# One load moves ahead of three others in the load queue: linear attention and two gated layers on one core

## The chip, the cores and the metric

The kernel runs on 1 core of a Trainium2 chip. The metric is the time of one execution on the device in microseconds (us), lower is better. The kernel before took 664.3 us (median of 3 runs, 663.88 to 666.28).

## The reference

Three stages follow each other: linear attention with decays over 4 batches of 8 heads and 768 positions, then two gated feed-forward layers over the 3072 resulting rows of 256.

```python
cum = np.cumsum(la, axis=-1)                      # la = log of the decays a of one chunk
L = np.exp(cum[..., :, None] - cum[..., None, :]) * causal
y = einsum(einsum(C, B) * L, x) + einsum(C, state) * exp(cum)
state = exp(sum(la)) * state + sum_j(B_j x_j * exp(cum[-1] - cum_j))
...
h = sigmoid(y @ w_gate) * (y @ w_val)
z = h @ w_out
...
g = z @ w2_in
out = (g * sigmoid(g)) @ w2_out
```

The reference works in chunks of 32 positions. The kernel takes chunks of 128, which gives the same sums.

## The kernel before

**Attention.** The 4 batches have 6 chunks of 128 positions each, so there are 24 chunks, numbered 0 to 23. For a chunk q the SP queue loads `bc` (B and C), `x` and `L`, the decays of all 8 heads broadcast over 128 partitions (`at_loadL`, L252, 512 KB into an `L` tile of 4 buffers). VectorE (DVE) turns the decays into the matrix L by one scan (`at_L`, L338), and GpSimd (POOL) makes `bw` from its last column (`at_bw`, L346). From chunk 4 on B and C are split in three bf16 parts by POOL (L298, L306), copied into the staging tiles `st` by ScalarE (ACT, L325) and DVE (L323), and transposed by two DMAs of the SP queue (`tr`, L327). TensorE (PE) multiplies the parts to `cb` in two halves (L381), DVE multiplies each half into L (L383), and PE makes `y` (L392 the part from the state, L398 the part within the chunk). ACT and DVE split y into `xT` (L450, L451), the input of the first gated layer.

**First gated layer.** Its 12 weight blocks f (gate, val and out) are loaded raw by three DMAs each (`w1_load`, L198 and L202, into a `raw` tile of 4 buffers), converted (`conv`: ACT L175 and L176, DVE L177 and L178, POOL L183 and L185, ACT L187, DVE L188; for the out part of the first seven blocks also `w1_split`, L221 and L222) and then used by PE (`g`, `v`: L509; `acc`: L558). The rows are taken in 7 row blocks of 2, 2, 4, 4, 4, 4, 4 chunks (`BLOCKS`). Row blocks 0 and 1 run together while the weights arrive; row block 2 (chunks 4 to 7) and later ones have all weights. DVE multiplies gate and value (`sg`, L530).

**Order of the work.** The program is written out by Python lists and then ordered by a scheduler, engine by engine. The SP queue keeps the order in which the loads are written. Two tables set that order: `WPOS` says before which attention step (an index into `ast`) each of the 31 steps of loading, converting and marking weight blocks (`wst`) is put, `RUNS` says how many steps are taken between the matmul groups. A tile's load waits until the last reader of the tile that had its buffer is done.

The lines that the text speaks of: a step with the position 31 is put ahead of attention step 31, one with 32 ahead of step 32.

```python
for i, g in enumerate(ast):
    steps += [w for w, p in zip(wst, WPOS) if p == i] + [g]
```

Of the kernel before, what the change touches and what calls it, by code (L numbers as in the profile page):

```python
# [30 lines left out]


WPOS = [
    0, 0, 0, 22, 25, 31, 31, 31, 31, 31, 31, 31, 32, 32, 32, 32, 32, 32, 32, 32, 32, 34, 34, 34, 34, 34, 35,
    35, 35, 35, 35,
]

# [865 lines left out]
```

## Time and profile before

| what | value |
|---|---|
| median of 3 runs | 664.3 us (663.88 to 666.28) |
| the profiled execution, its own time | 663.99 us |
| its span, first to last instruction | 662.2 us |
| PE busy | 635.5 us (96%) |
| DVE busy | 432.8 us (65%) |
| ACT busy | 329.0 us (50%) |
| POOL busy | 108.7 us (16%) |
| mean granted clock of PE | 0.992 of full speed |

Times in the profile are us from the start of the span. The execution's own time is 1.8 us above the span. Busy time is the sum of an engine's instructions. In the timelines a row is an instruction, or several alike in a row, with its start, how long it lasted, and in brackets how long the engine had stood idle before it and what ended that.

### The profile page before, as it was taken

What the parts mean: (1) busy time and instruction counts of PE and PEld (TensorE: products, weight loads), DVE (VectorE), ACT (ScalarE), POOL (GpSimd) and SP (SyncE); (2) the same over time, 40 slices, a digit from 0 to 9 for tenths busy, and PEclk for the clock granted to TensorE, in tenths of its full rate; (3) what the DMA queues carried; (4) which work ended last, traced back from release to release, by engine and by line L of the source; (5) the groups of instructions that cost most, each with busy time, mean ns of one, the idle gap of its engine ahead of it and who ended that gap; (6) DMA issues with size and microseconds to landing.
All of it is one profiled execution on the core that took longest, in us unless ns stands there. A gap on an engine that the chain in (4) does not pass through costs nothing.

```text
span 662.2 us, 9861 instructions
## 1 busy us (share of the span) xinstructions
PE 635.5 (96%) x3680; PEld 522.0 (79%) x3682; DVE 432.8 (65%) x660; ACT 329.0 (50%) x649; POOL 108.7 (16%) x129
## 2 busy tenths in 40 slices
PE   5788898999999999999999999999999999999998
PEld 2477796777778787787888878888888888888886
DVE  8988987676768578656348885564564655544644
ACT  5675554544544554434336664544554544444543
POOL 4555432211221222311002410000000000000000
PEclk9998999999999999999999999999999999999999
DMA  8958577774656365342002410000000000000000
GB/s 207 267 146 212 89 158 154 153 128 109 120 121 145 77 145 119 81 125 75 0 1 66 157 33 1 1 32 1 1 32 1 1 32 1 33 0 1 33 0 33
DMA packets 140145, 51.18 MB, mean 77 GB/s; under 512 B 119009, under 2 KB 133537, under 8 KB 140097
## 3 DMA queue, kind: packets, MB, share of 16 engines
q1 hardware_dynamic: 139952, 50.41, 32.1%
q8 instruction: 29, 0.48, 0.3%
q14 instruction: 20, 0.16, 0.1%
q10 hardware_dynamic: 144, 0.13, 0.1%
HBM read 36.80 MB, written 3.24 MB: 60 GB/s over the span
## 4 chain that ended last, share of the span: by engine, by line
PE 79%; DVE 4%; DMA 4%; issue 3%; POOL 2%; ACT 1%; SPq 0%; DVEq 0%; POOLq 0%; ACTq 0%
PE h L509 20%; PE o L807 13%; PE v L509 11%; PE acc L558 11%; PE g L509 11%; PE o L828 7%; DMA raw<-in_moe_w_out_dram 3%; PE y L398 2%; DMA L<-ac_d 1%; POOL cvt L185 1%; PE cb L381 1%; PE y L392 1%; DVE sg L530 1%; DVE cvt L178 1%; DVE L L338 1%
## 5 line engine op out<-in xcount | busy, mean ns | idle before, releaser
L509 PE MATMUL v<-xT,w 128*128 128x512 f32 (+1 forms) x504 | 119.4, 369 | 3.9 <-ACT sg L522 2.4
L509 PE MATMUL g<-xT,w 128*128 128x512 f32 (+1 forms) x504 | 120.8, 370 | 0.0
L782 DVE TENSOR_TENSOR sh<-h,sh 128x512 f32<-128x512 f32 x96 | 66.2, 691 | 63.2 <-ACT sh L781 61.7
L509 PE MATMUL h<-x2T,w2b 128*128 128x512 f32 x432 | 107.0, 389 | 0.0
L791 DVE TENSOR_TENSOR gl<-sh,gh 128x512 fp32r<-128x512 f32 x96 | 65.8, 690 | 58.4 <-ACT gh L786 56.9
L509 PEld LDWEIGHTS v<-xT,w 128*128 128x128 f32 x504 | 87.4, 192 | 19.3 <-ACT sg L522 3.0
L509 PEld LDWEIGHTS g<-xT,w 128*128 128x128 f32 x504 | 87.7, 191 | 16.3 <-issue 1.5
L558 PE MATMUL acc<-gh,w 128*128 128x512 f32 (+1 forms) x280 | 94.5, 380 | 0.2 <-ACT x1T L569 0.2
L781 ACT ACTIVATE sh<-h 128x512 f32<-128x512 f32 x96 | 57.5, 599 | 73.3 <-PE h L509 70.2
L509 PEld LDWEIGHTS h<-x2T,w2b 128*128 128x128 f32 x432 | 80.7, 188 | 16.5
L786 ACT CAST gh<-sh 128x512 fp32r<-128x512 f32 x96 | 59.0, 620 | 62.2 <-PE o L807 31.0
L503 ACT CAST gh<-sg 128x512 fp32r<-128x512 f32 (+1 forms) x70 | 41.2, 588 | 93.6 <-DVE sg L530 93.6
L807 PE MATMUL o<-w2b,gh 128*128 128x512 f32 x280 | 74.2, 390 | 0.0
L530 DVE TENSOR_TENSOR sg<-v,sg 128x512 f32<-128x512 f32 (+1 forms) x84 | 50.8, 607 | 30.4 <-PE v L509 29.5
L539 DVE TENSOR_TENSOR gl<-sg,gh 128x512 fp32r<-128x512 f32 (+1 forms) x70 | 50.6, 723 | 23.3 <-ACT gh L503 23.0
L338 DVE TENSOR_TENSOR_SCAN L<-L,eye 128x1024 f32<-128x1024 f32 x24 | 55.2, 2302 | 16.0 <-DMA L<-ac_d 15.9
L185 POOL TENSOR_TENSOR cvt<-cvt,raw 128x512 int32<-128x512 int32 (+1 forms) x28 | 46.5, 1664 | 98.7 <-DVE cvt L178 81.5
L522 ACT ACTIVATE sg<-g 128x512 f32<-128x512 f32 (+1 forms) x84 | 44.8, 534 | 31.5 <-PE g L509 28.6
L558 PEld LDWEIGHTS acc<-gh,w 128*128 128x128 f32 x280 | 52.3, 190 | 9.9 <-ACT x1T L569 0.3
L807 PEld LDWEIGHTS o<-w2b,gh 128*128 128x128 f32 x280 | 51.8, 188 | 10.3
L558 PE MATMUL acc<-gl,w 128*128 128x512 f32 (+1 forms) x140 | 53.3, 380 | 1.0 <-DVE gl L539 1.0
L828 PEld LDWEIGHTS o<-w2b,gl 128*128 128x128 f32 x288 | 36.9, 191 | 1.3
(95 smaller groups left out, 724.9 us busy)
## 6 DMA issues: line engine op xcount, KB each, us to landing
L<-ac_d SPq DMA_DIRECT2D x23, 512.0 KB, 4.7
raw<-in_moe_w_out_dram SPq DMA_DIRECT2D x28, 256.0 KB, 3.9
raw<-in_moe_w_in_dram SPq DMA_DIRECT2D x16, 256.0 KB, 2.8
x<-in_x_dram SPq DMA_DIRECT2D x24, 128.0 KB, 3.1
raw<-in_moe_w_gate_dram SPq DMA_DIRECT2D x12, 256.0 KB, 4.4
raw<-in_moe_w_val_dram SPq DMA_DIRECT2D x12, 256.0 KB, 4.7
out_dram<-o2t SPq DMA_DIRECT2D x20, 128.0 KB, 1.7
bc<-in_B_dram SPq DMA_DIRECT2D x24, 64.0 KB, 2.7
```

What stands on the lines that cost most here:

```text
L185: nc.gpsimd.tensor_tensor(ti, ti, r, ALU.add)
L338: nc.vector.tensor_tensor_scan(t["Lf"], t["Lf"], eye, 0.0, op0=ALU.mult, op1=ALU.add)
L509: nc.tensor.matmul(psum[:, :n], w[:, i, o + k * P : o + (k + 1) * P], xt[j][:, k, :n], start=(z == 0), stop=(z == len(k_terms) - 1),)
L530: nc.vector.tensor_mul(sg[:, :n], ps[:, :n], sg[:, :n])
L539: nc.vector.tensor_sub(lo[:, :n], sg[:, :n], hi[:, :n].bitcast(F32))
L558: mm = nc.tensor.matmul(o, v[:, ms], g[:, :n], start=(f == 0 and z == 0 and not (small and m)), stop=(f == NF1 - 1 and z == len(terms) - 1 ...
L781: nc.scalar.activation(sg, ps, AF.Sigmoid)
L782: nc.vector.tensor_mul(sg, ps, sg)
L786: nc.scalar.copy(hi, sg)
L791: nc.vector.tensor_sub(lo, sg, hi.bitcast(F32))
L807: nc.tensor.matmul(ps, hi[:, s], w2(f)[:, :, DM:], start=(f == 0), stop=False, skip_group_check=True,)
L828: nc.tensor.matmul(ps[:, :DM], g2[b, f][2][:, s], w2(f)[:, 0, DM:], start=False, stop=(f == NF2 - 1), skip_group_check=True,)
```

## The change

Nine numbers of `WPOS` go from 32 to 33.

```diff
 WPOS = [
-    0, 0, 0, 22, 25, 31, 31, 31, 31, 31, 31, 31, 32, 32, 32, 32, 32, 32, 32, 32, 32, 34, 34, 34, 34, 34, 35,
+    0, 0, 0, 22, 25, 31, 31, 31, 31, 31, 31, 31, 33, 33, 33, 33, 33, 33, 33, 33, 33, 34, 34, 34, 34, 34, 35,
     35, 35, 35, 35,
 ]
```

The nine steps are three conversions, three loads and three marks. Attention step 32 is the load of the decays of chunk 4, so that load is now written ahead of them.

The SP queue, from the load of x of chunk 4 on. `x_494` is that x; `L_551` before and `L_505` now is the tile of the decays of chunk 4; `raw_514`, `raw_535`, `raw_547` (now `raw_516`, `raw_537`, `raw_549`) are the weight blocks 7, 8 and 9. Before:

```order
 L273 DMA x_494<-in_x_dram 128x8x32
-L198 DMA raw_514<-in_moe_w_gate_dram 128x2x256
-L198 DMA raw_514<-in_moe_w_val_dram 128x2x256
-L202 DMA raw_514<-in_moe_w_out_dram 128x512
-L198 DMA raw_535<-in_moe_w_gate_dram 128x2x256
-L198 DMA raw_535<-in_moe_w_val_dram 128x2x256
-L202 DMA raw_535<-in_moe_w_out_dram 128x512
-L198 DMA raw_547<-in_moe_w_gate_dram 128x2x256
-L198 DMA raw_547<-in_moe_w_val_dram 128x2x256
-L202 DMA raw_547<-in_moe_w_out_dram 128x512
-L252 DMA L_551<-ac_d 128x1024
+L252 DMA L_505<-ac_d 128x1024
```

The load of the decays stood behind nine load instructions of three weight blocks, and now stands right behind the load of x; the nine follow it in their old order.

The scheduler moves work on the other engines too. DVE, where the scan of chunk 4 stands now (`w_105` are the converted weights, `st` the staging of chunk 4, `cvt_478` the conversion of block 4):

```order
 L178 SCALAR_TENSOR_TENSOR cvt_478<-raw_420,cvt_478 128x768
 L451 TENSOR_TENSOR xT_1_413<-y_432,xT_1_412 128x2x128
+L338 SCALAR_TENSOR_TENSOR L_505<-L_505,eye 128x1024
 L222 TENSOR_TENSOR w_105<-x1T,w_105 128x256
 L188 TENSOR_TENSOR w_105<-cvt_445,w_105 128x512
 L323 COPY st_617<-bc_615 128x8x32
 L323 COPY st_623<-bc_615 128x8x2x16
```

The scan stood 21 instructions further on, behind the conversion of block 7 (`cvt_539`), and now comes ahead of the weight splits and the staging copies of chunk 4. In the same way the scan of chunk 5 (`L_640`) now comes behind the staging copies of that chunk's B and C (`st_668`, `st_674`) instead of ahead of them.

DVE, some 50 instructions later, at the staging copies of chunk 6 (`st_760`, `st_766`) and the scan of chunk 6 (`L_707`):

```order
+L383 TENSOR_TENSOR L_640<-cb_1_722,L_640 128x512
+L338 SCALAR_TENSOR_TENSOR L_707<-L_707,eye 128x1024
+L188 TENSOR_TENSOR w_105<-cvt_598,w_105 128x768
 L530 TENSOR_TENSOR sg_7_1172<-v_7_1174,sg_7_1172 128x256
-L383 TENSOR_TENSOR L_640<-cb_0_709,L_640 128x512
-L188 TENSOR_TENSOR w_105<-cvt_598,w_105 128x768
 L323 COPY st_760<-bc_737 128x8x32
 L323 COPY st_766<-bc_737 128x8x2x16
```

Here the scan went the other way: it stood behind the staging copies of chunk 6, and now stands ahead of them, with the last weight conversion and a gate product between.

On PE the matmuls of the state of chunk 4 (L414) move up, behind the products of row block 1 with weight block 1, and those of `cb` of chunk 5 move up ahead of the gate matmuls of row block 1 with weight block 7. On POOL `bw` of chunk 4 moves up ahead of the conversion of weight block 5. On DVE the second multiply of `cb` into L of chunk 7 (L383) now stands ahead of the low part of `xT` of chunk 6 (L451); both stand behind the scan of chunk 8, and `y` of chunk 7 (L392) waits for that part. After row block 2 the orders are as they were, but for a few rows.

## Rows read from the trace of the kernel before

**Rows 1.** The page, part 1: busy us (share of the span) and instructions.

```profile
PE 635.5 (96%) x3680; PEld 522.0 (79%) x3682; DVE 432.8 (65%) x660; ACT 329.0 (50%) x649; POOL 108.7 (16%) x129
```

**Rows 2.** Busy time by stretch: PE, PEld, DVE, ACT, POOL, then clock, DMA share, GB/s.

```profile
40.00:62.00 22.00, 17.58 (x116) 15.62 (x115) 18.06 (x25) 15.54 (x30) 13.65 (x12) 0.99 0.60 174
62.00:112.00 50.00, 44.40 (x391) 39.89 (x391) 45.07 (x71) 25.07 (x59) 17.21 (x19) 0.94 0.70 136
112.00:350.00 238.00, 238.00 (x1447) 188.86 (x1447) 152.33 (x236) 107.50 (x219) 45.67 (x61) 1.00 0.46 101
```

**Rows 3.** Timeline of PE, two places at which it waited.

```profile
61.04 1.33 PE L509 MATMUL v<-xT,w 128*128 128x256 f32 x6 [2.36 <-ACT sg L522]
...
109.81 0.71 PE L392 MATMUL y<-cwT,S 128*128 128x128 f32 x4 [1.61 <-DVE xT L451]
```

**Rows 4.** Timeline of the SP queue: start, duration of the issue.

```profile
37.13 2.12 SPq L273 DMA_DIRECT2D x<-in_x_dram  x1
43.99 0.37 SPq L198 DMA_DIRECT2D raw<-in_moe_w_gate_dram  x1
...
52.72 0.37 SPq L198 DMA_DIRECT2D raw<-in_moe_w_gate_dram  x1
...
54.15 0.43 SPq L252 DMA_DIRECT2D L<-ac_d  x1
```

**Rows 5.** Tile L, 10 to 125 us: load to landing, min, median, max.

```profile
DMA to landing us min/median/max: 4.2/4.8/6.5
```

**Rows 6.** Timeline of DVE around the old and the new place of the scan.

```profile
41.66 0.42 DVE L451 TENSOR_TENSOR xT<-y,xT 128x256 fp32r<-128x256 f32 x1 [0.49 <-ACT xT L450]
43.17 1.07 DVE L222 TENSOR_TENSOR w<-x1T,w 128x256 fp32r<-128x256 f32 x1 [1.08 <-ACT w L221]
...
45.26 2.04 DVE L323 COPY st<-bc 128x256 bf16<-128x256 bf16 x2
47.22 0.41 DVE L530 TENSOR_TENSOR sg<-v,sg 128x256 f32<-128x256 f32 x1
...
60.64 2.29 DVE L338 TENSOR_TENSOR_SCAN L<-L,eye 128x1024 f32<-128x1024 f32 x1 [1.93 <-DMA L<-ac_d]
```

**Rows 7.** Timeline of POOL; the first row ran beside the scan of DVE at 29.65.

```profile
29.86 2.60 POOL L183 TENSOR_TENSOR x1T<-cvt,raw 128x256 int32<-128x256 int32 x1 [1.75 <-DMA raw<-in_moe_w_out_dram]
...
41.97 0.73 POOL L183 TENSOR_TENSOR x1T<-cvt,raw 128x256 int32<-128x256 int32 x1
...
45.89 1.32 POOL L185 TENSOR_TENSOR cvt<-cvt,raw 128x512 int32<-128x512 int32 x1
...
73.05 0.61 POOL L306 TENSOR_TENSOR bc<-bcr 128x256 bf16<-128x256 f32 x1
```

**Rows 8.** Timeline of ACT: the waits for the raw weights.

```profile
48.77 0.94 ACT L176 ACTIVATE raw<-raw 128x768 int32<-128x768 uint32 x1 [0.62 <-DMA raw<-in_moe_w_out_dram]
...
59.04 0.89 ACT L176 ACTIVATE raw<-raw 128x768 int32<-128x768 uint32 x1 [2.23 <-DMA raw<-in_moe_w_out_dram]
```

**Rows 9.** Timeline of DVE, 69 to 92 us: scans, staging copies and what lies between.

```profile
78.25 1.94 DVE L323 COPY st<-bc 128x256 bf16<-128x256 bf16 x2
...
86.58 0.69 DVE L383 TENSOR_TENSOR L<-cb,L 128x512 f32<-128x512 f32 x1 [0.26 <-PE cb L381]
87.39 0.96 DVE L188 TENSOR_TENSOR w<-cvt,w 128x768 fp32r<-128x768 f32 x1
88.26 0.36 DVE L323 COPY st<-bc 128x256 bf16<-128x256 bf16 x2
...
89.60 2.29 DVE L338 TENSOR_TENSOR_SCAN L<-L,eye 128x1024 f32<-128x1024 f32 x1 [0.31 <-DMA L<-ac_d]
```

**Rows 10.** Timeline of the SP queue: transposes of chunk 5, decays and transposes of chunk 6.

```profile
80.12 2.58 SPq L327 DMA_TRANSPOSE tr<-st  x2
...
84.63 0.69 SPq L252 DMA_DIRECT2D L<-ac_d  x1
88.63 2.58 SPq L327 DMA_TRANSPOSE tr<-st  x2
```

## The prediction

> **What bounds the kernel now.** I read the page first: PE is busy for 96% of the span [rows 1], so a change can only give back some of its 26.7 us of idle time, or add to it. Then busy time by stretch, to see where that idle time lies [rows 2]. From 112 to 350 us PE is busy without a gap; from 40 to 62 us it lacks 4.4 us (22.00 − 17.58), from 62 to 112 us 5.6 us. In these two stretches DVE is busier than PE (18.06 and 45.07 us against 17.58 and 44.40), and POOL is busiest in the first. The change lies here: weights are converted by ACT, DVE and POOL while row blocks 0 and 1 use them, and attention prepares chunks 4 to 7 for row block 2.
>
> Then PE's own waits [rows 3]. At 61.04 it had waited 2.36 us for ACT, which had waited 2.23 us for a raw weight block [rows 8]. At 109.81 it had waited 1.61 us for the split of chunk 6's y on DVE, in the attention chain that ends where row block 2 can begin. What sets the end is thus how early this chain is through; behind it PE is full.
>
> That chain has a rhythm of its own on the SP queue [rows 10]: the transposes of chunk 5 are issued at 80.12, those of chunk 6 at 88.63, 8.5 us later, because B and C of the next chunk are loaded behind the transposes of this one and must pass POOL, ACT and DVE before they can be transposed.
>
> **The change, part by part.**
>
> *The load.* x of chunk 4 is issued at 37.13 and takes 2.12 us to issue, then SP waits until 43.99 for a raw buffer [rows 4]. The decays' load now falls into that hole, at 39.3; its issue takes 0.43, so the weight loads behind it lose nothing. Loads of decays land 4.2 to 6.5 us after issue, median 4.8 [rows 5]. I take 4.8: landing at 44.1, 43.5 to 45.8. Weight block 9, issued at 52.72, loses a neighbour: the decays followed it at 54.15, and it was there at 59.04, 6.3 us on, where the block issued at 43.99 was there at 48.77, 4.8 us on [rows 4, 8]. Worth 1.5 us to it.
>
> *The scan.* It is not left where it was. DVE comes to it at 42.08, behind the row at 41.66 [rows 6], finds the data missing until 44.1, scans for 2.29 and is free at 46.4, where it began the next instruction at 43.17: 3.2 us late. At 60.64 it saves the scan and 1.93 us of wait, together 4.2 us.
>
> How much of the 3.2 us reaches the product at 47.22? The two staging copies took 2.04 us beside POOL [rows 6], against 0.36 at 88.26 [rows 9]; if POOL is done by then, 1.7 us come back, and 0.4 us of waits shrink: 1.1 us late. But POOL cannot run on beside a scan: its instruction at 29.86 took 2.60 us beside one, against 0.73 without [rows 7]. So its work of 44 to 47 us is pushed behind the scan and meets the copies again: 3.2 us. Between 1.1 and 3.2 I take 2.0; with a landing at 45.8 the upper end is 4.9.
>
> *Weights.* DVE's and POOL's conversions from 47 us on shift by 2.0, and so does the raw buffer that frees block 9's load: issued at 54.7, there at 59.5 with 4.8 us instead of 59.04. PE's wait at 61.04 ends 0.5 us later (−0.4 to +1.7 for 1.1 to 3.2). This lies ahead of the chain below, beside it, and does not add to it.
>
> *Chunk 5.* SP goes on behind the last weight loads, which are late by 2.0 like POOL. So B and C of chunk 5 are late by 2.0, and POOL's last step for them ends at 75.7 instead of 73.66 (73.05 + 0.61 [rows 7]). The copies of chunk 5 no longer stand behind a scan, and DVE has the 4.2 us in hand: they run at once, for 0.36 to 1.94 us [rows 9], middle 1.15. The transposes go out at 76.8 instead of 80.12, 3.3 us early.
>
> *Chunk 6.* This gain meets the other move. The copies of chunk 6 now stand behind the scan of chunk 6, whose data are loaded behind the transposes of chunk 5. From 80.12 to the issue of that load at 84.63 and to the scan at 89.60 [rows 9, 10] it is 9.5 us. From 76.8 that gives 86.3; scan 2.29, weight split 0.87, product 0.33 (starts a little closer than durations, 0.96 and 0.41 [rows 6, 9]), copies 0.36: 90.1, against 88.63 before. The transposes of chunk 6 are 1.5 us late. With 1.1, 3.2 and 4.9 us above: 0.6, 2.7 and 4.4.
>
> *To row block 2.* The chain from there on keeps its 8.5 us. On DVE a multiply of 0.69 us [rows 9] is new ahead of the split that PE waited for at 109.81; it costs between nothing and 0.7, I take 0.3. PE's other moves only change the order of matmuls that all run, at nothing; their cover is the queue of row blocks 0 and 1's products, and without it they would cost what the chain costs already. Behind 112 us PE is full and the loss stays.
>
> *Sum.* +1.5 + 0.3 = +1.8 us on the profiled execution's 663.99 (span 662.2, 1.8 us around it), which lies 0.3 below the median of 664.3: **665.8 us**.
>
> One rule speaks for the change. The Trainium skill (DMA: Bandwidth & Descriptors, section "Rules for kernel authors") advises to issue a transfer early, compute, and wait for it late, so that its cost is covered. The rows show the load earlier, but the wait earlier too: 2.0 us of it at 42 us in place of 1.93 at 60.64 [rows 6]. By the rule alone the sum would be 663.99 − 1.93 = 662.1.
>
> **The rivals.**
>
> *Faster: the early load is pure gain.* The 4.2 us that DVE saves at 60.64 carry through, and the 3.3 us that chunk 5 gains last. For it: DVE is the busiest engine from 62 to 112 us [rows 2], and block 9 loses a neighbour. Against it: the copies of chunk 6 now stand behind a scan whose data come 9.5 us behind the transposes. Time: 663.99 − 3.3 = 660.7. The Trainium skill (DMA: Bandwidth & Descriptors, "Rules for kernel authors") points to this side. Chance 0.08.
>
> *No change: the chain has slack.* PE waited only 1.61 us at 109.81, and with its own queue of row blocks 0 and 1 late as well, both losses may cover each other. Time 664.0 to 664.3. Chance 0.20, with 0.02 of it for a change that does not do what it says, because SP would be held at the load until 43.99 anyway; no buffer speaks for that, since chunk 0, whose buffer is used, was finished long before 37 us.
>
> *Slower: the scan blocks DVE in earnest.* The load lands 6.5 us after issue, like the worst one [rows 5], because small packets of x are still in the queue at 39.3, and POOL is inside an instruction of 1.32 us [rows 7] when the data come. Then DVE is late by 4.9 at 47.22 instead of 2.0, and everything behind it by 2.9 more: 665.8 + 2.9 = 668.7. It passes half a per cent from about 3.8 us of lateness on. For it: DVE has no idle time to catch up in. Chance 0.27.
>
> **How the numbers follow.** Forecast 0.45, between +0.6 and +3.4 us (lateness 1.1 to 3.2, with 0 to 0.7 at the end): 664.6 to 667.4. A measurement tells half a per cent, 3.3 us, from no change: 661.0 to 667.6. So within it lie the forecast and the second rival, 0.65; slower 0.27; faster 0.08. The range leaves out most of the faster rival and the far end of the slower one: 662.1 to 669.0.
>
> **What would show it.** In the timeline of DVE, the scan of chunk 4 at about 44.1 behind a wait of some 2 us for the decays; the first product of row block 1 at about 49.2; no wait for the decays near 60. The transposes of chunk 5 near 76.8 and those of chunk 6 near 90.1. PE full from about 114 us on, with the same 238 us for the stretch behind. Wrong would be: chunk 6's transposes ahead of 88, a gap in PE behind 115 us, or a scan at 42 without a wait.

## The result and the profile after

The changed kernel takes **670.13 us** (median of 4 runs, 669.25 to 671.43), the kernel before beside it 664.33 (4 runs): ratio 1.0086, 95% interval 1.0063 to 1.0109. It is slower by 5.8 us, where 665.8 was forecast. The profiled execution, the slowest of its four, took 671.43.

The page, part 1, and then busy time by stretch, with the columns of [rows 2]:

```profile
PE 640.6 (96%) x3680; PEld 524.1 (78%) x3682; DVE 433.4 (65%) x660; ACT 328.6 (49%) x649; POOL 115.2 (17%) x129
```

```profile
40.00:62.00 22.00, 18.18 (x120) 16.09 (x119) 19.60 (x29) 13.90 (x28) 14.09 (x13) 0.92 0.54 169
62.00:112.00 50.00, 42.94 (x355) 38.50 (x353) 39.70 (x62) 25.57 (x58) 18.98 (x18) 0.93 0.62 127
112.00:350.00 238.00, 235.34 (x1442) 185.41 (x1443) 152.87 (x238) 105.11 (x215) 49.72 (x62) 0.99 0.47 103
```

Beside [rows 1, 2]: from 62 to 112 us PE does 36 fewer instructions and is busy for 1.5 us less, and DVE is busy for 39.7 us instead of 45.1. Work has moved out to the right, past 112 us, where PE was busy without a gap before and now lacks 2.7 us (238.00 − 235.34).

The SP queue (start, duration of the issue), against [rows 4, 10]:

```profile
36.81 1.80 SPq L273 DMA_DIRECT2D x<-in_x_dram  x1
38.66 0.58 SPq L252 DMA_DIRECT2D L<-ac_d  x1
43.28 0.37 SPq L198 DMA_DIRECT2D raw<-in_moe_w_gate_dram  x1
...
54.36 0.37 SPq L198 DMA_DIRECT2D raw<-in_moe_w_gate_dram  x1
...
78.10 2.58 SPq L327 DMA_TRANSPOSE tr<-st  x2
...
82.60 0.58 SPq L252 DMA_DIRECT2D L<-ac_d  x1
92.29 2.59 SPq L327 DMA_TRANSPOSE tr<-st  x2
```

The load sits in the hole that the prediction named. The transposes of chunk 5 are 2.0 us earlier than in [rows 10], those of chunk 6 **3.66 us later**: 14.2 us apart, where it was 8.5.

DVE, four pieces: the scan of chunk 4, the copies and scan of chunk 5, what stands ahead of the copies of chunk 6 (91.94), and the two instructions behind the scan of chunk 8. They answer to [rows 6, 9]:

```profile
43.39 2.58 DVE L338 TENSOR_TENSOR_SCAN L<-L,eye 128x1024 f32<-128x1024 f32 x1 [1.87 <-DMA L<-ac_d]
...
48.40 0.56 DVE L323 COPY st<-bc 128x256 bf16<-128x256 bf16 x2
48.89 0.41 DVE L530 TENSOR_TENSOR sg<-v,sg 128x256 f32<-128x256 f32 x1
...
76.16 2.01 DVE L323 COPY st<-bc 128x256 bf16<-128x256 bf16 x2 [0.51 <-POOL bc L306]
78.09 2.28 DVE L338 TENSOR_TENSOR_SCAN L<-L,eye 128x1024 f32<-128x1024 f32 x1
...
83.74 2.01 DVE L539 TENSOR_TENSOR gl<-sg,gh 128x256 fp32r<-128x256 f32 x1
...
86.27 0.41 DVE L539 TENSOR_TENSOR gl<-sg,gh 128x256 fp32r<-128x256 f32 x1
...
87.95 0.69 DVE L383 TENSOR_TENSOR L<-cb,L 128x512 f32<-128x512 f32 x1 [0.93 <-PE cb L381]
88.56 2.28 DVE L338 TENSOR_TENSOR_SCAN L<-L,eye 128x1024 f32<-128x1024 f32 x1
90.75 0.93 DVE L188 TENSOR_TENSOR w<-cvt,w 128x768 fp32r<-128x768 f32 x1
91.60 0.42 DVE L530 TENSOR_TENSOR sg<-v,sg 128x256 f32<-128x256 f32 x1
91.94 0.35 DVE L323 COPY st<-bc 128x256 bf16<-128x256 bf16 x2
...
113.96 0.67 DVE L383 TENSOR_TENSOR L<-cb,L 128x512 f32<-128x512 f32 x1
114.54 0.41 DVE L451 TENSOR_TENSOR xT<-y,xT 128x256 fp32r<-128x256 f32 x1
```

POOL beside it: the last step for the values of chunk 6 (L306) ends at 87.15, so the copies of 91.94 waited 4.8 us for nothing but their turn on DVE. The last row is `bw` of chunk 8, behind the scan of that chunk.

```profile
43.79 2.72 POOL L183 TENSOR_TENSOR x1T<-cvt,raw 128x256 int32<-128x256 int32 x1
...
83.62 1.85 POOL L185 TENSOR_TENSOR cvt<-cvt,raw 128x768 int32<-128x768 int32 x1 [5.67 <-DMA bc<-in_B_dram]
...
86.30 0.85 POOL L306 TENSOR_TENSOR bc<-bcr 128x256 bf16<-128x256 f32 x1
...
114.19 0.41 POOL L346 TENSOR_TENSOR bw<-bc,L 128x128 f32<-128x128 f32 x1 [4.81 <-DVE L L338]
```

PE, its waits, and the first matmul of row block 2 (the first of 512 columns):

```profile
49.35 1.65 PE L509 MATMUL v<-xT,w 128*128 128x256 f32 x6 [2.79 <-DVE sg L530]
...
80.74 0.98 PE L509 MATMUL v<-xT,w 128*128 128x256 f32 x6 [2.50 <-DVE sg L530]
...
83.87 1.65 PE L509 MATMUL g<-xT,w 128*128 128x256 f32 x6 [1.18 <-DVE sg L530]
...
114.66 0.44 PE L414 MATMUL st<-x,bw 128*32 128x64 f32 x8 [3.06 <-POOL bw L346]
115.10 1.19 PE L392 MATMUL y<-cwT,S 128*128 128x128 f32 x4
...
118.82 0.63 PE L509 MATMUL g<-xT,w 128*128 128x512 f32 x1
```

In the kernel before, the same row of the same view of PE reads:

```profile
112.49 0.47 PE L509 MATMUL g<-xT,w 128*128 128x512 f32 x1
```

Row block 2 begins 6.33 us later. This row turned out to be the number to read. In the profiles of all 15 kernels of this study the execution's own time less this start is 551.5 to 553.5 us, so all but 2 us of the differences is made ahead of it. The table has the starts of the transposes of chunks 5 and 6 and of row block 2 and the execution's own time (us, from one profiled execution each), then the median of all runs and the ratio of times from them (before = 1). The kernel before was run again beside each series: 664.27 us beside e, 665.36 beside f, 664.72 beside g, 665.12 beside h.

| kernel | chunk 5 | chunk 6 | row block 2 | own time | median (runs) | ratio, 95% interval |
|---|---|---|---|---|---|---|
| before | 80.12 | 88.63 | 112.49 | 663.99 | 664.30 (3) | 1 |
| changed | 78.10 | 92.29 | 118.82 | 671.43 | 670.13 (4) | 1.0086 (1.0063 to 1.0109) |
| e1_load_only | 81.18 | 89.83 | 113.67 | 666.01 | 665.43 (12) | 1.0009 (0.9998 to 1.0020) |
| e2_order_to_78 | 77.04 | 87.51 | 110.91 | 662.95 | 665.89 (12) | 1.0013 (0.9999 to 1.0026) |
| e3_order_to_95 | 79.52 | 93.71 | 117.65 | 671.04 | 669.60 (6) | 1.0076 (1.0056 to 1.0096) |
| e4_order_to_119 | 78.56 | 92.75 | 118.42 | 670.29 | 670.02 (4) | 1.0087 (1.0073 to 1.0102) |
| f1_scan6_behind_staging | 79.27 | 91.28 | 116.76 | 669.83 | 669.83 (5) | 1.0071 (1.0055 to 1.0087) |
| f2_splits_behind_product | 78.73 | 92.38 | 116.87 | 669.90 | 670.84 (6) | 1.0087 (1.0066 to 1.0108) |
| f3_both_moves | 77.77 | 88.68 | 115.34 | 668.85 | 668.69 (12) | 1.0052 (1.0037 to 1.0068) |
| f4_before_order_78_to_95 | 79.35 | 90.08 | 115.57 | 669.09 | 667.90 (10) | 1.0037 (1.0025 to 1.0049) |
| g1_filled_waits | 78.85 | 92.25 | 116.84 | 670.01 | 669.95 (6) | 1.0074 (1.0059 to 1.0090) |
| g2_staging6_first | 80.56 | 90.23 | 116.45 | 668.57 | 665.60 (12) | 1.0013 (1.0000 to 1.0026) |
| g3_only_78_to_95 | 79.88 | 93.35 | 117.64 | 669.96 | 670.83 (6) | 1.0092 (1.0074 to 1.0109) |
| h1_moves_then_before | 79.44 | 90.37 | 115.39 | 667.61 | 667.57 (10) | 1.0036 (1.0023 to 1.0050) |
| h2_scan6_ahead_only | 77.66 | 90.81 | 114.90 | 667.41 | 669.73 (6) | 1.0069 (1.0052 to 1.0086) |

A profile is one execution, and executions of one kernel differ by up to 5.2 us here (f3): that of e2 is near the fastest of its 12 runs (662.73 to 667.62, median 665.89), that of h2 is the fastest of its 6, those of the changed kernel and of g2 are the slowest of theirs. Sizes below are therefore from medians and ratios, with 0.1% as 0.66 us; the profiles tell the mechanism. The expectations are written for a kernel before of 664.3 us, so for the series f, g and h a ratio times 664.27 is held against them.

### The profile page after: what moved, and what is told of

Its sections match the earlier page's. It is cut to its first block, busy times and chain, and to the rows that moved or that the text cites. A ratio compares the mean times of both kernels' runs of the same rounds, so it can differ in the third digit from the quotient of the medians.

```text
span 669.7 us, 9861 instructions
## 1 busy us (share of the span) xinstructions
PE 640.6 (96%) x3680; PEld 524.1 (78%) x3682; DVE 433.4 (65%) x660; ACT 328.6 (49%) x649; POOL 115.2 (17%) x129
## 4 chain that ended last, share of the span: by engine, by line
PE 78%; DMA 3%; DVE 3%; issue 2%; POOL 1%; ACT 1%; SPq 0%; ACTq 0%; POOLq 0%; DVEq 0%
PE h L509 20%; PE o L807 13%; PE v L509 11%; PE acc L558 11%; PE g L509 11%; PE o L828 7%; DMA raw<-in_moe_w_out_dram 2%; PE y L398 2%; DMA L<-ac_d 2%; PE cb L381 1%; PE y L392 1%; POOL cvt L185 1%; DVE gl L539 1%; PE st L414 1%; DVE L L338 0%
## 5 line engine op out<-in xcount | busy, mean ns | idle before, releaser
L503 ACT CAST gh<-sg 128x512 fp32r<-128x512 f32 (+1 forms) x70 | 41.2, 589 | 87.7 <-DVE sg L530 87.6
L539 DVE TENSOR_TENSOR gl<-sg,gh 128x512 fp32r<-128x512 f32 (+1 forms) x70 | 51.0, 729 | 29.0 <-ACT gh L503 28.6
L185 POOL TENSOR_TENSOR cvt<-cvt,raw 128x512 int32<-128x512 int32 (+1 forms) x28 | 46.2, 1652 | 99.9 <-DVE cvt L178 79.5
L383 DVE TENSOR_TENSOR L<-cb,L 128x512 f32<-128x512 f32 x48 | 32.8, 683 | 8.3 <-PE cb L381 6.9
```

The costliest lines, as they stand in the source:

```text
L185: nc.gpsimd.tensor_tensor(ti, ti, r, ALU.add)
L539: nc.vector.tensor_sub(lo[:, :n], sg[:, :n], hi[:, :n].bitcast(F32))
```

## The experiments

The change moves one DMA in the program, but the scheduler then writes another order for DVE, ACT, PE and POOL. To take the two apart, a list of instructions was fixed for each of these engines by edges that order and make no wait between engines:

```diff
-    w1stack.close()
+    w1stack.close(); _pin(tc)
...
+def _pin(tc):
+    by = {i.name: i for i in tc.nc.cur_bb.bb.instructions}
+    for line in _PIN.values():
+        names = [n for n in ("I-" + k for k in line.split()) if n in by]
+        for p, n in zip(names, names[1:]):
+            tc.add_manual_dep(by[n], p, NOSYNC, reason="pin")
```

Both orders were cut at the same places of the program (at the scan of chunk 5, some 78 us; at 95 us; at row block 2, 119 us), so that each piece can be taken from either kernel.

**e1: the load alone.** `WPOS` as changed, `_PIN` the order of before on all four engines.

> The load of the decays of chunk 4 stands where the change puts it, and DVE, ACT, PE and POOL keep the order of instructions of the kernel before. Theory O (order): the loss comes from the new order on the engines, so this gives 662.1 to 664.6, and the scan of chunk 4 runs at 60 to 61 us with nothing to wait for. Theory L (load): the earlier transfer itself costs, by what it delays on the queues, so this gives 669 to 671.

Measured 665.43 us beside 664.27 of before, ratio 1.0009. DVE's timeline shows the scan of chunk 4 with no wait:

```profile
58.68 2.28 DVE L338 TENSOR_TENSOR_SCAN L<-L,eye 128x1024 f32<-128x1024 f32 x1
```

The row had 1.93 us of wait in [rows 6]. The load is early, its wait is gone, and the time is the same. Theory L falls by 3.6 us. The loss comes with the new order, as theory O has it, but the time is 0.8 us above O's range, which had counted on a gain from the wait. So the early transfer costs at most 0.2% and gives nothing either. The reverse, the load in its old place with the new order, was not tried: the scan of chunk 4 would wait on DVE for a load that itself waits for weight steps behind that scan.

**e2, e3, e4: the changed order, piece by piece.** The load as changed; the order of the changed kernel up to 78, 95 and 119 us, that of before behind.

```diff
-_PIN = before
+_PIN = changed[: cut] + before[cut :]
```

> The load as changed; the four engines keep the changed kernel's order up to the scan of chunk 5 (about 78 us there), and the order of before behind it. Theory O1 (the early scan of chunk 4, its wait at 42 us and what it displaces, is the loss): 668.5 to 670.5. Theory O2 (the loss is made behind 80 us, where the scan of chunk 6 has been put behind the multiplies of chunk 5): 664 to 666.5, since the on-record sum gave the first part +1.8 at the most. Theory L: 669 to 671.

> As the run before it, but with the changed order kept up to 95 us (the chunk 6 piece too), and that of before behind it. O2: 667.5 to 669.5, 2.5 to 4 more than with the changed order up to 78 us only, the transposes of chunk 6 at 91 to 92.5 us. O1: 668.5 to 670.5 and within 0.7 of that run.

> As the run before it, with the changed order kept up to the first row-block-2 matmuls at about 119 us, and that of before behind it. If the step to row block 2 (an extra multiply ahead of the split of xT, the state matmuls ahead of those of y) costs as the traces say (1.73 longer from the scan of chunk 8 to the first matmul): 1 to 2 more than the run with the changed order up to 95 us, and within 0.7 of the changed kernel (669.4 to 670.8). If the cost of that step is only the slow clock of one profile: within 0.5 of the run with the order changed up to 95 us, and the rest is lost behind 119 us.

Measured 665.89, 669.60 and 670.02 us. The early scan of chunk 4 with all that it displaces costs 0.5 us against e1 (665.43), less than the measurement tells. The piece from 78 to 95 us costs 3.7 (4.2 by the ratios), the next one 0.4, and the rest nothing. O1 falls. O2 names the right piece, though e3 came out 0.1 us above its range and, in the profile, with the transposes of chunk 6 at 93.71 instead of 91 to 92.5. The step to row block 2 costs less than the 1 to 2 us expected of e4, and nothing is lost behind 119 us. In e2, POOL has the data of the copies of chunk 6 at 86.42 (85.81 + 0.61), DVE comes to the copies 0.7 us later, and scans behind them. POOL and DVE of e2:

```profile
82.36 2.79 POOL L185 TENSOR_TENSOR cvt<-cvt,raw 128x768 int32<-128x768 int32 x1 [5.47 <-DVE cvt L178]
85.11 0.61 POOL L298 TENSOR_TENSOR bcr<-bc 128x256 f32<-128x256 f32 x1
85.81 0.61 POOL L306 TENSOR_TENSOR bc<-bcr 128x256 bf16<-128x256 f32 x1
```

```profile
87.16 0.35 DVE L323 COPY st<-bc 128x256 bf16<-128x256 bf16 x2
...
88.09 2.28 DVE L338 TENSOR_TENSOR_SCAN L<-L,eye 128x1024 f32<-128x1024 f32 x1
```

In e3 the two stand the other way round, as in the changed kernel:

```profile
89.36 0.69 DVE L383 TENSOR_TENSOR L<-cb,L 128x512 f32<-128x512 f32 x1 [0.93 <-PE cb L381]
89.97 2.28 DVE L338 TENSOR_TENSOR_SCAN L<-L,eye 128x1024 f32<-128x1024 f32 x1
...
93.35 0.36 DVE L323 COPY st<-bc 128x256 bf16<-128x256 bf16 x2
```

**f1 to f4: what in the piece from 78 to 95 us.** Two theories: S, the scan ahead of the copies; K, TensorE's waits at 80.74 and 83.87 us and the half clock behind them. f2 makes the first of these moves on DVE of the changed kernel, f1 the second, f3 both; f4 puts the whole piece back, on all four engines:

```diff
 L383 multiply of chunk 4, second half
+L530 sg_8    L539 gl_7
 L188 w<-cvt_590    L178 cvt_598
-L530 sg_8    L539 gl_7
...
 L383 multiply of chunk 5, second half
-L338 scan of chunk 6
 L188 w<-cvt_598    L530 sg_7    L323 st (chunk 6) x2
+L338 scan of chunk 6
```

> The changed kernel with one move on DVE: the scan of chunk 6 goes behind the weight split, the product and the two staging copies of chunk 6 that now stand behind it. Theory S (the scan of 2.28 ahead of the staging copies delays the transposes of chunk 6, and the chain keeps that): 667 to 668.5, the transposes of chunk 6 some 2 earlier than the 92.3 of the changed kernel. Theory K (the loss of this stretch is TensorE's: it waits for a product at 82.7 us and then runs at half the clock until 90 us): 669.3 to 670.5, no less.

> The changed kernel with one move on DVE: the last steps of two weight splits (0.94 each, at 81.67 and 82.54 us) go behind the product and the split of the value path that now stand behind them. Theory K: the product comes 1.9 earlier, PE's wait of 1.18 at 83.87 us goes and with it the half clock up to 90 us (10 us of matmuls at half speed, some 3 lost), so 666 to 668, granted clock 1.00 between 80 and 90 us. Theory S: 669.3 to 670.5, since the scan still stands ahead of the staging copies.

> The changed kernel with both of these moves. Theory S and K each give the lower of the two single moves here; if the causes are separate and add up, 664.5 to 666.5.

> The changed kernel with the four engines' order of before between the scan of chunk 5 and 95 us, and its own order ahead of that and behind it. If the stretch is worth the 3.7 that the first series gave it, and nothing behind it undoes that: 665.7 to 667.2. If what follows (from 95 us on) costs as much by itself whatever comes ahead: 668.5 to 670.

Measured ratios 1.0071, 1.0087, 1.0052 and 1.0037 (before 665.36 in this series). Against 664.27 that is 669.0, 670.1, 667.7 and 666.7 us. Putting the whole piece back is worth 3.3 us (1.0086 − 1.0037), as f4's first case has it. f2 gives nothing, against theory K; it is no clean test of it, as its move also sends POOL's last weight step from 83.62 to 84.92 us, and the granted clock from 80 to 90 us rises only from 0.66 to 0.83. f1 gives 1.0 us, which lies between the ranges of the two theories; both moves give 2.3, less than f3's 664.5 to 666.5. The intervals of f1 and of the changed kernel overlap, so f1 alone decides nothing. Its profile shows where the gain went: the transposes of chunk 6 follow those of chunk 5 after 12.0 us instead of 14.2, but then those of chunk 7 follow after 10.0 (91.28 to 101.27) instead of 8.8, because the multiply ahead of the copies of chunk 7 starts no earlier than in the changed kernel (99.97, there 99.82): DVE stood idle 0.44 us for PE's `cb` of chunk 6:

```profile
99.97 0.69 DVE L383 TENSOR_TENSOR L<-cb,L 128x512 f32<-128x512 f32 x1 [0.44 <-PE cb L381]
...
100.91 0.35 DVE L323 COPY st<-bc 128x256 bf16<-128x256 bf16 x2
```

**g1: TensorE's waits filled.** 23 matmuls of zeros into a sum that they don't change, in the two waits:

```diff
-    ZO = {}
+    ZO = {(0, 6, 1, 0): 16, (0, 7, 0, 0): 7}
```

> The changed kernel, all orders as they are, with 23 more matmuls of zeros (added to a sum that they leave as it is): 16 in PE's wait of 2.50 at 78.2 us, 7 in its wait of 1.18 at 82.7 us. Theory K (the half clock that follows these waits is most of the loss between 78 and 95 us): granted clock 1.00 between 80 and 95 us and 666.5 to 668.5. Theory S (the chain through DVE's scan and the staging copies of chunk 6 holds whatever the clock does): the clock is 1.00, the transposes of chunk 6 are at 91 to 92.5 us still, and the time is 669.3 to 670.5.

The stretch from 78 to 95 us, of the changed kernel and then of g1:

```profile
78.00:95.00 17.00, 12.96 (x91) 11.45 (x91) 15.34 (x25) 6.53 (x16) 4.44 (x4) 0.80 0.45 95
```

```profile
78.00:95.00 17.00, 14.76 (x129) 12.92 (x128) 16.47 (x26) 7.21 (x17) 5.13 (x5) 1.00 0.48 96
```

The clock column goes from 0.80 to 1.00, PE's two waits shrink to 0.80 and 0.39 us, the transposes of chunk 6 stay (92.25), and the time is 669.95 us (664.72 before, ratio 1.0074), within the changed kernel's interval; against 664.27 it is 669.2, 0.1 below theory S's range and 0.7 above theory K's. As most of the loss, theory K falls: the low clock went with TensorE's waits for products of DVE, and shortening the waits with the clock at 1.00 gave 0.8 us, no more than the noise. A smaller cost of the clock, inside the intervals, is not excluded.

**g2: POOL's turn.** From e2: POOL's last weight step (L185, 2.79 us there) behind the values of chunk 6, copies first on DVE and ACT.

```diff
 POOL
-L185 cvt_598
 L298 bcr (chunk 6)    L306 bc (chunk 6)
+L185 cvt_598
```

> From the kernel with the load as changed, the changed order up to 78 us and that of before behind it (665.9): POOL's two steps for the values of chunk 6 go ahead of its step for the last weight block (which takes 2.79 there and holds them), DVE's staging copies and ACT's follow, and the last weight split's steps on ACT and DVE go behind. If the chain that passes the transposes of chunk 6 (87.5 us there) sets the end and keeps what it is given: transposes of chunk 6 at 85 to 86 and 663 to 664.8. If the end is set elsewhere: 665.3 to 666.5. If the later weight block is then what PE waits for: 666.5 to 669.

Measured 665.60 (664.72 before, ratio 1.0013): no different from e2, and against 664.27 it is 665.1, between the first two cases. The weight step that was sent behind now runs beside the copies, on POOL and on DVE:

```profile
87.57 0.61 POOL L306 TENSOR_TENSOR bc<-bcr 128x256 bf16<-128x256 f32 x1
88.14 1.86 POOL L185 TENSOR_TENSOR cvt<-cvt,raw 128x768 int32<-128x768 int32 x1
```

```profile
88.22 2.00 DVE L323 COPY st<-bc 128x256 bf16<-128x256 bf16 x2 [0.61 <-POOL bc L306]
```

In this profile POOL has the values of chunk 6 7.6 us behind the transposes of chunk 5 (88.18 − 80.56), where e2 had 9.4. The copies then take 2.00 us instead of 0.35, so what was gained on POOL is lost on DVE, and the transposes come at 90.23, not at the 85 to 86 expected. The test of the chain stays inconclusive.

**g3: the piece without the early scan.** The order of before, but for the piece from 78 to 95 us.

> The load as changed, with the order of before on the four engines but for the stretch from the scan of chunk 5 to 95 us, which keeps the changed order. If that stretch costs its 3.3 to 3.7 whatever the first part does: 668.5 to 670. If it costs only where the scan of chunk 4 runs early (it was put together by the scheduler for that case): 665 to 667.

Measured 670.83 (664.72 before, ratio 1.0092). The piece costs 5.5 us against e1 even where the scan of chunk 4 is late, more than the 3.3 to 3.7 expected: it is bad by itself, not by what comes ahead of it.

**h1, h2: the scan's place by itself.** h1 is e3 with both moves of f3. h2 is e2 with a single move, which puts the scan ahead of the copies as f1 put it behind them; five short instructions come behind it:

```diff
 L383 multiply of chunk 5, first half
+L338 scan of chunk 6
 L188 w<-cvt_598    L323 st (chunk 6) x2    L539 gl_7    L530 sg_8
-L338 scan of chunk 6
```

> The changed order up to 95 us with both moves in it (the two weight split steps behind the product, the scan of chunk 6 behind the staging copies), and the order of before behind 95 us; without the two moves that gave 669.6. If the places of these three instructions make the loss of the stretch: 665.7 to 667.2, transposes of chunk 6 3 us earlier. If the earlier matmuls of chunk 5 on TensorE, which are left where the change has them, make it: 668.7 to 670.

> The changed order up to 78 us and that of before behind it (665.9), with one move on DVE: the scan of chunk 6 goes ahead of the weight split and the staging copies of chunk 6, as in the changed kernel. If the scan's place by itself delays the transposes by its 2.28 and the chain keeps that: 667.5 to 668.7, transposes of chunk 6 2 to 2.5 later than 87.5. If it needs the other moves of the stretch: 665.5 to 666.7.

h1: 667.57 (665.12 before, ratio 1.0036), 2.7 us less than e3; against 664.27 it is 666.7, in the range for the places of the three instructions. h2: 669.73, ratio 1.0069, which is 3.7 us more than e2 (0.56% of 664.7), with intervals well apart; against 664.27 it is 668.9, 0.2 above the range for the scan's place by itself. DVE and the SP queue of h2:

```profile
86.54 0.69 DVE L383 TENSOR_TENSOR L<-cb,L 128x512 f32<-128x512 f32 x1 [0.46 <-PE cb L381]
87.17 2.29 DVE L338 TENSOR_TENSOR_SCAN L<-L,eye 128x1024 f32<-128x1024 f32 x1
89.38 0.93 DVE L188 TENSOR_TENSOR w<-cvt,w 128x768 fp32r<-128x768 f32 x1
90.22 0.57 DVE L323 COPY st<-bc 128x256 bf16<-128x256 bf16 x2
```

```profile
90.81 2.58 SPq L327 DMA_TRANSPOSE tr<-st  x2
```

The transposes of chunk 6 come 13.2 us behind those of chunk 5, where e2 had 10.5. One instruction of 2.28 us, put ahead of the two copies, is enough for a loss as large as that of the whole piece. Of the five instructions behind it, the copies are the ones that the transposes follow at once; PE waited 0.61 us for the split of a product (L539), and the five were not tried apart. The reverse is weaker: putting it back in the changed kernel (f1) gave 1.0 us, within noise, and with the second move 2.3 there and 2.7 in h1. So the parts of the piece do not add up. h1 stays 1.5 us above e2 with the piece's other moves on PE, ACT and DVE left in it, the earlier `cb` matmuls of chunk 5 among them; they were not tried by themselves, and their share is not shown.

## Why the prediction was wrong

**What bounds the kernel: right.** The time follows the start of row block 2 to within 2 us in 15 profiles, and behind it PE is full: in the changed kernel it is busy for all of the 231 us from 119 to 350.

**The load, the scan, the weights: right.** Issued at 38.66 (39.3 forecast) and there by 43.39 (44.1). DVE waited 1.87 us for it and was free at 45.97 (46.4); the product of 47.22 came at 48.89 (49.2), and block 9's load at 54.36 (54.7). POOL's L183 beside the scan took 2.72 us, as [rows 7] had it with 2.60. Not forecast: that late product made PE wait 2.79 us at 49.35, where it had waited 0.41 for it before, and the wait of 2.36 at 61.04 is gone in return. All of this costs 0.5 us in e2 against e1, no more than noise.

**Chunk 5: too large a gain.** POOL's last step ended at 76.13 (75.7). The transposes went out at 78.10 (76.8), because the copies took 2.01 us beside a POOL step, the upper end given instead of the middle. So chunk 5 gained 2.0 us, not 3.3. What such a head start is worth stays open. The profile of e2 has it (77.04, and 81.18 in e1), its chunk 6 is 2.3 us ahead of e1's and that execution is 3.1 us shorter; but over all runs e2 is no faster than e1 (665.89 and 665.43). In e2 the values of chunk 6 stand on POOL behind a weight step of 2.79 us.

**Chunk 6: the step that failed.** "This gain meets the other move": the scan ahead of the copies was named and its place was right, but both sides of the balance were mis-sized. The forecast put the transposes of chunk 6 13.3 us behind those of chunk 5 (90.1 − 76.8), 4.8 more than the 8.5 of before, and set the gain of 3.3 against it, which left 1.5. Measured were 14.2 us, 5.7 more, against a gain of 2.0, which left 3.66. The longer way comes from the scan: it was forecast to be held by its data, 9.5 us behind the transposes of chunk 5, which is 87.6 from the measured 78.10. Its data were there at 87.0 (issued at 82.60, landed 4.4 us later), and it started at 88.56, held by its turn, behind a multiply that waited 0.93 us for PE's `cb` of chunk 5, which the change had put ahead as well. The prediction had not counted that multiply there. In the runs no gain shows to set against the loss: the order up to 78 us makes e2 no faster than e1, the piece from 78 to 95 us costs 3.7 us behind it, and h2 has 3.7 us for the scan's place alone.

**To row block 2: too small.** 0.3 us was forecast. In the profile it took 26.5 us instead of 23.9 from the transposes of chunk 6 to row block 2. PE's moves were put at nothing, but the state's matmuls, which now stand ahead of those of y, waited 3.06 us for POOL's `bw` behind the scan of chunk 8, and the matmuls behind ran at 1.2 GHz (granted clock 0.50 from 115.1 to 118.6 us; y 1.19 us for 0.71). The extra multiply of 0.67 us did not set y's start: the split behind it ended at 114.95, the state's matmuls at 115.10. By medians the order from 95 to 119 us costs 0.4 us behind e3, and about 1.6 (1.0037 − 1.0013) with what follows where the piece ahead is that of before.

**The sum.** In place of +1.5 and +0.3 the medians of one series give 1.2 for the load (0.6 by the ratio), 0.5 for the order up to 78 us, 3.7 up to 95 and 0.4 up to 119: together 5.8 (670.02 − 664.27), the loss of the changed kernel. Of these four only the 3.7 is clear of noise. No kernel here was faster than the kernel before.

**The rivals.** Faster: falls; neither the load alone (e1) nor the load with the new order up to 78 us (e2) is faster. Taking away the wait of 1.93 us gave nothing: e1 is at 665.43, where 662.1 had been worked out from that wait. No change by slack in the chain: falls, with h2; 2.7 us more from chunk 5 to chunk 6 in its profile go with 3.7 us in the time. Slower by a late landing: the sign was right, not the mechanism; the load landed 4.7 us after its issue, near its median.

## What to carry to other kernels

In a kernel that a scheduler orders, a moved load is two changes; hold the order fixed and move the load alone before believing a price for either. Before a gain on one link of a chain is set against a loss on the next, list every instruction that stands ahead of the next link in the new order: here a multiply was missed, and the gain was smaller than counted. On an engine that feeds a queue, try the short copies that the queue waits for ahead of a long instruction whose result is needed later: the wrong order cost 3.7 us in h2, though in the changed kernel, which had other moves as well, putting it right gave 1.0 us, within noise.

## What the runs showed of the hardware

Short DVE instructions that began behind the start of a POOL step could last until just behind its end: in the changed kernel the split of a product (128x256) took 2.01 us at 83.74 and ended at 85.75, the POOL step at 85.47, against 0.41 us at 86.27; in g2 the copies took 2.00 us and ended at 90.22, the POOL step at 90.00, against 0.35 in e2. The Trainium skill (SBUF — State Buffer, section "Who interferes with whom") says that the two engines share a port pair as an exclusive lock, for a DVE instruction with two SBUF inputs beside one of GpSimd that reads; the split is such a one, and the trace agrees. In g2 a gain on POOL was lost on DVE in this way.

Not expected either: 6 us of TensorE at 1.2 GHz (granted clock 0.50 from 83.87 to 90 us, behind waits of 2.50 and 1.18 us) cost nothing that showed. With the waits filled and the clock at 1.00 the ratio moved from 1.0086 to 1.0074, inside both intervals. The low clock marked a place where PE had waited; it was not most of what the piece costs.
